# Retention and Fourier-mix kernel: the first batch's k and v loaded by casting transfers from GpSimd

## The chip, the cores and the metric

The kernel runs on one core of a Trainium2 chip. The metric is the device time of one execution in microseconds; lower is better. The core has five engines with their own instruction queues: TensorE (PE in the profile; PEld is its weight load), VectorE (DVE), ScalarE (ACT), GpSimd (POOL) and SyncE (SP), which here only issues transfers. Each runs its own list in order and waits on semaphores. Transfers go through 16 DMA engines, fed from a hardware queue (SP's) and a software queue (GpSimd's).

## The reference

Two stages. The first is a recurrence with decay over 768 steps, for 4 batches and 8 heads of width 64. The second adds the real part of a two-dimensional Fourier transform, normalizes, and runs an MLP of width 2048 with a residual.

```python
def _attn_ref(q, k, v):                       # (4, 8, 768, 64), float32
    gamma = 1.0 - 2.0 ** (-5.0 - np.arange(H))
    scale = 1.0 / np.sqrt(D)
    for t in range(S):
        state = gamma[None, :, None, None] * state + np.einsum('bhd,bhe->bhde', k[:, :, t], v[:, :, t])
        y[:, :, t] = scale * np.einsum('bhd,bhde->bhe', q[:, :, t], state)
    return y

def _moe_ref(x, w_ch1, w_ch2):                # x: (4, 768, 512)
    X = np.fft.fft(np.fft.fft(x, axis=1), axis=2)
    u = x + np.real(X).astype(np.float32)
    mu, var = np.mean(u, axis=-1, keepdims=True), ...
    un = (u - mu) / np.sqrt(var + 1e-06)
    return u + np.maximum(un @ w_ch1, 0.0) @ w_ch2
```

## The kernel before

**The recurrence in chunks.** The 768 steps are cut into 6 chunks of 128 (`NCH`, `P`), and heads are taken in pairs, four pairs to a batch, in the order 0, 1, 3, 2. Within a chunk the output is a masked product of q and k times v. Between chunks a 64 x 64 state per head is carried. The decay is split over the operands: `gkd` scales k by gamma^(127 - j) for row j of a chunk, `gq8` scales the output by gamma^(i + 1)/8 for row i. A product of q with the scaled k therefore carries a factor gamma^(128) too much between rows i and j, and the masked eviction (L471) multiplies by gamma^(-128) and by a mask of zeros and ones, `maskf`.

**A head pair of the first batch** goes through these units, each a small function:

- `load_unit` (L158) sends q, k and v of the pair from SP (L165), each 384 KB in float32, into the pool `inp` of 11 buffers. For q of the first two batches a partition holds six consecutive steps ("h (p c) d"), which makes rows of 1536 bytes in memory. For k and v a partition holds one step of each chunk ("h (c p) d"), which makes rows of 64 floats, 256 bytes. All four pairs' loads are issued at the start.
- `q0_unit` (L394) casts q to float16 on GpSimd. `k0_unit` (L402) scales and casts k into `kd` on GpSimd, one instruction a head; for the last pair the second head goes to ScalarE (L414). `v0_unit` (L418) casts v on GpSimd; for the last pair half of it goes to VectorE (L427).
- `t0_unit` (L430) transposes q (part 0) or the scaled k (part 1) on TensorE, six 128 x 128 transposes each, and `te_unit` (L442) copies the result out of PSUM on ScalarE.
- `am_unit` (L453) multiplies k and q per chunk (12 small matmuls), and `ae_unit` (L468) is the masked eviction on VectorE, four instructions a pair, into `atm`.
- `kv0_unit` (L477) multiplies the scaled k and v into the chunk states, `sc_unit` (L490) carries them through the chunks with one scan on VectorE.
- `yi_unit` and `yx_unit` (L501, L515) add both parts of the output in PSUM, and `x0_unit` (L531) writes them to `x` on ScalarE.

Between these stand units that build the Fourier tables: `ts_dve` and `td_dve` (L296, L305: three VectorE instructions each, L288 to L292), `t_act` and `csn_unit` on ScalarE. `filler` (L148) issues matmuls whose result is not used. `w1_unit` and `w2_unit` (L990, L998) load the MLP's weights: eight transfers from GpSimd which read float32 in rows of 512 floats and write float16.

**Order.** The order of the first batch is a list written by hand, `first_units` (L1037), and `pin` (L104) fixes it on every engine: an instruction can't pass the one ahead of it in the list on the same engine. GpSimd's constants (L198 to L222, L339 to L347) stand ahead of the whole list. After that the four batches' work is woven from streams with due times in units of one batch's MLP (`emit`, L1092), where only GpSimd's order is fixed. The order of SP's loads and transposes among these streams is set by a scheduler with a cost model, which knows when a buffer comes free.

**Later batches.** `cast_unit` (L361) does the casts on GpSimd for all later batches. The second batch's loads wait for the seventh weight transfer and for the matmuls of `h0_unit(1, 3)` (L166 to L171); loads of batches 2 and 3 wait for the matmuls of the pair a batch earlier (L172). Batches 2 and 3 transpose q and k by transfers on SP (L548, L550), and un as well (L916), so that SP's queue carries loads, transposes and the output's stores.

Of the kernel before, what the change touches and what calls it, by code (L numbers as in the profile page):

```python
# [18 lines left out]
P = 128  # L19
# [24 lines left out]
def kernel(  # L44
# [17 lines left out]
    inp = pool("inp", 11)  # L62
# [116 lines left out]

    for i in range(4):  # L180
        load_unit(0, i)()
# [5 lines left out]
    gexp = const.tile([P, 2, H], f32, tag="gexp")  # L187
    gq8, gkd = gexp[:, 0], gexp[:, 1]
# [15 lines left out]
    for h in range(H):  # L204
# [6 lines left out]
                            op0=ALU.mult)  # L211
    nc.scalar.activation(gexp, gexp, AF.Exp, bias=0.0, scale=1.0)
# [146 lines left out]
    at, q16_of, kd_of, v16_of, last_cast = {}, {}, {}, {}, {}  # L359

    def cast_unit(b, i):  # L361
        def run():
# [3 lines left out]
            v16 = vp.tile([P, NCH, 2, D], f16, tag="v16", name="v16")  # L366
            with ExitStack() as es:
# [14 lines left out]
                for h2 in range(2):  # L382
# [6 lines left out]
                    out=v16, in0=v32.rearrange("p h c d -> p c h d"), scalar1=1.0, scalar2=1.0,  # L389
# [11 lines left out]

    def k0_unit(i):  # L402
        def run():
            h0 = 2 * PAIR_ORDER[i]
            k32 = in_of.pop(("k", 0, i))
            kd = kd_of[0, i] = kp.tile([P, NCH, 2, D], f16, tag="kd16", name="kd16")
            nc.gpsimd.tensor_scalar(out=kd[:, :, 0, :], in0=k32[:, 0], scalar1=gkd[:, h0:h0 + 1],  # L407
                                    scalar2=1.0, op0=ALU.mult, op1=ALU.mult)
            if i < 3:
                nc.gpsimd.tensor_scalar(out=kd[:, :, 1, :], in0=k32[:, 1],  # L410
                                        scalar1=gkd[:, h0 + 1:h0 + 2], scalar2=1.0,
                                        op0=ALU.mult, op1=ALU.mult)
            else:
                nc.scalar.activation(kd[:, :, 1, :], k32[:, 1], AF.Copy, bias=0.0,  # L414
                                     scale=gkd[:, h0 + 1:h0 + 2])
        return run

    def v0_unit(i):  # L418
        def run():
            v32 = in_of.pop(("v", 0, i)).rearrange("p h c d -> p c h d")  # L420
            v16 = v16_of[0, i] = vp.tile([P, NCH, 2, D], f16, tag="v16", name="v16")
            n = NCH if i < 3 else 3
            last_cast[0, i] = nc.gpsimd.tensor_scalar(
                out=v16[:, 0:n], in0=v32[:, 0:n], scalar1=1.0, scalar2=1.0, op0=ALU.mult,
                op1=ALU.mult)
            if n < NCH:
                nc.vector.tensor_copy(v16[:, n:], v32[:, n:])  # L427
# [754 lines left out]
```

## Time and profile before

| What | Value |
|---|---|
| Time, median of 3 runs | 247.18 us (246.52 to 247.30) |
| Profiled execution, first to last instruction (its span) | 245.4 us |
| TensorE busy | 234.2 us, 95% of the span, 2024 matmuls |
| VectorE busy | 177.0 us, 72% |
| ScalarE busy | 124.2 us, 51% |
| GpSimd busy | 81.7 us, 33% |
| Bytes read from memory | 27.26 MB |
| SP queue | 94960 packets, 31.86 MB |
| GpSimd queue (weights) | 4224 packets, 4.19 MB |

The profiled execution has its own span; what lies around the span is in the time and not in the trace, so the time is compared with the span plus the difference, 1.8 us here. Busy time is the sum over an engine's instructions, each with its own start and end. A group of the timeline is printed as: start, length, engine, line, operation, output and input with shapes, count, and in brackets the idle time ahead of it with what ended it. The granted TensorE clock is 1.00 throughout.

### The profile page before, as it was taken

How to read it: one execution, taken by the hardware profiler on the slowest of the kernel's cores; microseconds unless marked ns; L12 is line 12 of the kernel's file. 1: busy time of each engine (PE TensorE's matmuls, PEld its weight loads, DVE VectorE, ACT ScalarE, POOL GpSimd, SP SyncE). 2: the span in 40 equal slices, each digit the busy share in tenths (PEclk: the TensorE clock that was granted, in tenths of full speed). 3: DMA queues.
4: the chain of work that ended last, by engine and by line, in shares of the span. 5: the costliest groups of instructions: out<-in, count | busy, mean ns of one | idle time of the engine just before them, and what ended most of it. 6: DMA issues, size and time to landing. Idle time of an engine off the chain costs nothing.

```text
span 245.4 us, 5309 instructions
## 1 busy us (share of the span) xinstructions
PE 234.2 (95%) x2024; PEld 143.8 (59%) x2024; DVE 177.0 (72%) x430; ACT 124.2 (51%) x276; POOL 81.7 (33%) x146
## 2 busy tenths in 40 slices
PE   6997899999999998999999999999999999999995
PEld 2454668956776655665567546655666455445543
DVE  8997957897897788996885748887895656424112
ACT  8798669587775434751247414742247317202500
POOL 6667601465600057690000646660002405000000
PEclk9999999999999999999999999999999999999999
DMA  8999999699999377999999667786200241221012
GB/s 173 256 260 140 204 195 205 164 245 230 291 229 222 75 168 165 191 181 137 256 272 214 116 141 203 129 120 139 87 1 0 45 151 21 47 85 43 0 45 85
DMA packets 99209, 36.39 MB, mean 148 GB/s; under 512 B 89840, under 2 KB 96240, under 8 KB 99184
## 3 DMA queue, kind: packets, MB, share of 16 engines
q1 hardware_dynamic: 94960, 31.86, 62.2%
q0 software_dynamic: 4224, 4.19, 10.7%
q8 instruction: 16, 0.26, 0.5%
q14 instruction: 9, 0.07, 0.1%
HBM read 27.26 MB, written 6.29 MB: 137 GB/s over the span
## 4 chain that ended last, share of the span: by engine, by line
PE 71%; DMA 7%; DVE 7%; POOL 4%; ACT 4%; SPq 3%; issue 1%; POOLq 0%; ACTq 0%; DVEq 0%
PE psc L979 30%; PE psh L936 25%; DMA k<-in_k_dram 5%; PE ps L736 3%; SPq L165 3%; PE wkA L600 3%; DMA q<-in_q_dram 2%; PE wkY L654 2%; PE pq L833 2%; PE wkY L650 1%; POOL u L870 1%; PE wkK L619 1%; ACT un L885 1%; DVE bst L889 1%; POOL kd L407 1%
## 5 line engine op out<-in xcount | busy, mean ns | idle before, releaser
L979 PE MATMUL psc<-w,ht 128*128 128x512 f16 (+2 forms) x400 | 89.3, 371 | 0.0
L936 PE MATMUL psh<-unT,w 128*128 128x384 f16 x448 | 81.6, 326 | 0.4 <-ACT ht L940 0.2
L979 PEld LDWEIGHTS <-ht 128*128 128x128 f16 x400 | 37.5, 98 | 36.5 <-issue 0.2
L936 PEld LDWEIGHTS <-w 128*128 128x128 f16 x448 | 42.3, 98 | 24.7 <-issue 1.4
L940 ACT ACTIVATE ht<-psh 128x384 f16<-128x384 f32 x64 | 30.9, 489 | 41.7 <-PE psh L936 41.1
L870 POOL TENSOR_TENSOR u<-u,x 128x256 f32<-128x256 f32 x21 | 13.3, 635 | 100.3 <-DVE u L840 91.0
L983 DVE SCALAR_TENSOR_TENSOR ob<-psc,stats,u 128x512 f32<-128x512 f32 (+2 forms) x25 | 18.1, 726 | 26.1 <-PE psc L979 26.0
L942 DVE TENSOR_SCALAR ht<-psh 128x384 f16<-128x384 f32 x48 | 26.2, 548 | 7.7 <-PE psh L936 7.4
L603 DVE TENSOR_TENSOR atm<-wkA,maskp 128x512 f16<-128x512 f32 x36 | 23.8, 681 | 1.6 <-PE wkA L600 1.6
L891 ACT ACTIVATE un<-u,stats 128x512 f16<-128x512 f32 x21 | 15.2, 722 | 16.7 <-DVE stats L890 12.1
L889 DVE BATCH_NORM_STATS2 bst<-u 128x6 f32<-128x512 f32 x21 | 14.6, 694 | 7.7 <-POOL u L872 7.6
L629 DVE SCALAR_TENSOR_TENSOR s<-s,gk,wkK 128x128 f16<-128x128 f16 x48 | 16.3, 341 | 3.7 <-ACT s L625 2.7
L662 ACT ACTIVATE x<-wkY,gexp 128x384 f16<-128x384 f32 x24 | 12.8, 581 | 8.0 <-PE wkY L654 8.0
L151 PE MATMUL wps<-ht 128*128 128x512 f16 x40 | 13.5, 444 | 2.2 <-POOL ht L202 2.2
L383 POOL TENSOR_SCALAR kd<-k,gexp 128x384 f16<-128x384 f32 x24 | 13.8, 585 | 3.6 <-DMA k<-in_k_dram 3.6
L872 POOL TENSOR_TENSOR u<-u,x 128x256 f32<-128x256 f32 x21 | 13.3, 635 | 3.0 <-DVE stats L890 3.0
L600 PE MATMUL wkA<-qTz,kT 128*128 128x256 f16 x72 | 13.4, 273 | 0.1
L835 ACT COPY qn<-pq 128x128 f32<-128x128 f32 x18 | 4.9, 272 | 13.6 <-PE pq L833 13.6
L953 PE MATMUL psh<-unT,w 128*128 128x128 f16 x192 | 11.5, 219 | 0.1
L953 PEld LDWEIGHTS <-w 128*128 128x128 f16 x192 | 11.0, 98 | 0.7 <-issue 0.5
L840 DVE SCALAR_TENSOR_TENSOR u<-pq,g,qn 128x256 f32<-128x256 f32 x18 | 8.5, 472 | 3.3 <-PE psh L936 2.5
L388 POOL TENSOR_SCALAR v<-v 128x768 f16<-128x768 f32 x12 | 10.0, 831 | 1.3 <-DMA v<-in_v_dram 1.3
(164 smaller groups left out, 315.6 us busy)
## 6 DMA issues: line engine op xcount, KB each, us to landing
q<-in_q_dram SPq DMA_DIRECT2D x16, 384.0 KB, 6.3
k<-in_k_dram SPq DMA_DIRECT2D x16, 384.0 KB, 5.6
v<-in_v_dram SPq DMA_DIRECT2D x16, 384.0 KB, 6.3
out_dram<-ob SPq DMA_DIRECT2D x23, 256.0 KB, 2.6
w<-in_moe_w_ch_dram POOLq DMA_DIRECT2D x8, 512.0 KB, 10.8
unT<-un SPq DMA_TRANSPOSE x15, 2.4
out_dram<-ob SPq DMA_DIRECT2D x1, 192.0 KB, 1.9
qTz<-q16z SPq DMA_TRANSPOSE x8, 3.9
```

The source lines that it names most:

```text
L600: mm = nc.tensor.matmul(wk[:, c2], st["kT"][:, c, :], st["qT"][:, :, c, :], start=True, stop=True)
L603: nc.vector.tensor_tensor(out=st["atm"][:, 2 * part:2 * part + 2], in0=wk, in1=maskp[:, PAIR_ORDER[i]].unsqueeze(1).to_broadcast([P, 2, 2, ...
L629: nc.vector.scalar_tensor_tensor(out=s16[:, c], in0=s16[:, c - 1], scalar=gk2[:, hp:hp + 1], in1=wk[:, c - c0], op0=ALU.mult, op1=ALU.add)
L870: nc.gpsimd.tensor_tensor(out=u[:, kb, 0:256], in0=u[:, kb, 0:256], in1=x[:, kb, 0, 1:257], op=ALU.add)
L889: nc.vector.bn_stats(bst, u[:, kb, :])
L891: una = nc.scalar.activation(un, u[:, kb, :], AF.Identity, bias=stats[:, kb, 0:1], scale=-1.0)
L936: nc.tensor.matmul(psh, w116[:, cb, fb * P:(fb + 1) * P], unT[:, cb, rt * 384:(rt + 1) * 384], start=(cb == 0), stop=(cb == 3))
L940: nc.scalar.activation(ht16[:, fb, :], psh, AF.Relu, bias=0.0, scale=-1.0)
L942: nc.vector.tensor_scalar(out=ht16[:, fb, :], in0=psh, scalar1=-1.0, scalar2=0.0, op0=ALU.mult, op1=ALU.max)
L953: mm = nc.tensor.matmul(psh[:, f], w116[:, cb, fb * P:(fb + 1) * P], unT[:, cb, kb * P:(kb + 1) * P], start=(cb == 0), stop=(cb == 3))
L979: nc.tensor.matmul(psc[:, c0:c1], ht16[:, fb, rb3 * P:(rb3 + 1) * P], w216[:, fb, c0:c1], start=(fb == 0), stop=(fb == NFB - 1))
L983: nc.vector.scalar_tensor_tensor(out=ob[:, c0:c1], in0=psc[:, c0:c1], scalar=lb[b]["st"][:, rb, 3:4], in1=lb[b]["u"][:, rb, c0:c1], op0=AL ...
```

## The change

- k and v of the first batch are no longer loaded by SP. Each is loaded by one transfer per head pair issued from GpSimd, which reads float32 and writes float16. SP loads q alone (`q_load`).
- These eight transfers stand in GpSimd's list: `kl_unit(0)`, `kl_unit(1)`, `vl_unit(0)` and `kl_unit(2)` ahead of everything else of `first_units`, the others between later units.
- GpSimd's scaling of k and cast of v are gone for this batch, with the parts that ScalarE and VectorE had. `k0_unit` now scales the float16 k into `kd` on VectorE, two instructions a pair, behind k's transposes in the list.
- `t0_unit` transposes the unscaled float16 k, head by head, twelve half-width transposes in place of six. The decay that the scaled k carried into the product is put into the masked eviction: its factor is now `gkm`, gamma^-(j + 1) for row j, one number a partition, in place of the constant gamma^(-128). `gkm` is a third row of the table of exponents `gexp`.
- v16 is laid out head, chunk, width in place of chunk, head, width, in all batches; the matmuls that read it are changed alike.
- The pool of float32 inputs goes from 11 to 8 buffers; a pool of 4 float16 buffers for k is new.

```diff
@@ -59,7 +59,8 @@
         return ctx.enter_context(tc.tile_pool(name=name, bufs=bufs, **kw))
 
     const = pool("const", 1)
-    inp = pool("inp", 11)
+    inp = pool("inp", 8)
+    kin = pool("kin", 4)
     vp = pool("vp", 4)
     kp = pool("kp", 3)
     tp = pool("tp", 2)
@@ -177,15 +178,20 @@
                 in_of[name, b, i] = t
         return run
 
+    def q_load(i):
+        h0 = 2 * PAIR_ORDER[i]
+        t = in_of["q", 0, i] = inp.tile([P, 2, NCH, D], f32, tag="in32", name="q32")
+        nc.sync.dma_start(t, q[0, h0:h0 + 2].rearrange("h (p c) d -> p h c d", p=P))
+
     for i in range(4):
-        load_unit(0, i)()
+        q_load(i)
 
 
     icol_i = const.tile([P, 8], i32, tag="icol_i")
     icol = const.tile([P, 8], f32, tag="icol")
     lgrow = const.tile([P, H], f32, tag="lgrow")
-    gexp = const.tile([P, 2, H], f32, tag="gexp")
-    gq8, gkd = gexp[:, 0], gexp[:, 1]
+    gexp = const.tile([P, 3, H], f32, tag="gexp")
+    gq8, gkd, gkm = gexp[:, 0], gexp[:, 1], gexp[:, 2]
     ident16 = const.tile([P, P], f16, tag="ident16")
     tmp = up.tile([P, NCH, DM], f32, tag="u32", name="tmp")
     tmp2 = up.tile([P, NCH, DM], f32, tag="u32", name="tmp2")
@@ -209,6 +215,8 @@
                             scalar2=float(math.log(0.125)), op0=ALU.mult, op1=ALU.add)
     nc.vector.tensor_scalar(out=gexp[:, 1], in0=lgrow, scalar1=icol[:, 5:6], scalar2=None,
                             op0=ALU.mult)
+    nc.vector.tensor_scalar(out=gexp[:, 2], in0=lgrow, scalar1=icol[:, 3:4], scalar2=-1.0,
+                            op0=ALU.mult, op1=ALU.mult)
     nc.scalar.activation(gexp, gexp, AF.Exp, bias=0.0, scale=1.0)
     for h2 in range(2):
         nc.scalar.activation(gk2[D * h2:D * h2 + D], lgrow[D * h2:D * h2 + D, h2:H:2], AF.Exp,
@@ -356,14 +364,14 @@
     x_edges(0)()
 
 
-    at, q16_of, kd_of, v16_of, last_cast = {}, {}, {}, {}, {}
+    at, q16_of, kd_of, v16_of, last_cast, k16_of = {}, {}, {}, {}, {}, {}
 
     def cast_unit(b, i):
         def run():
             h0 = 2 * PAIR_ORDER[i]
             q32, k32, v32 = (in_of.pop((n, b, i)) for n in "qkv")
             kd = kp.tile([P, NCH, 2, D], f16, tag="kd16", name="kd16")
-            v16 = vp.tile([P, NCH, 2, D], f16, tag="v16", name="v16")
+            v16 = vp.tile([P, 2, NCH, D], f16, tag="v16", name="v16")
             with ExitStack() as es:
                 if b < NPE:
                     if (b, i - 1) in last_cast:
@@ -386,7 +394,7 @@
                     if b < NPE:
                         es.enter_context(tc.issue_after(kc.ins))
                 last_cast[b, i] = nc.gpsimd.tensor_scalar(
-                    out=v16, in0=v32.rearrange("p h c d -> p c h d"), scalar1=1.0, scalar2=1.0,
+                    out=v16, in0=v32, scalar1=1.0, scalar2=1.0,
                     op0=ALU.mult, op1=ALU.mult)
             q16_of[b, i], kd_of[b, i], v16_of[b, i] = q16, kd, v16
         return run
@@ -399,32 +407,31 @@
                 "p h c d -> p c h d"), scalar1=1.0, scalar2=1.0, op0=ALU.mult, op1=ALU.mult)
         return run
 
+    def kl_unit(i):
+        def run():
+            h0 = 2 * PAIR_ORDER[i]
+            k16_of[i] = kin.tile([P, 2, NCH, D], f16, tag="k16", name="k16")
+            nc.gpsimd.dma_start(k16_of[i],
+                                k[0, h0:h0 + 2].rearrange("h (c p) d -> p h c d", p=P))
+        return run
+
     def k0_unit(i):
         def run():
             h0 = 2 * PAIR_ORDER[i]
-            k32 = in_of.pop(("k", 0, i))
             kd = kd_of[0, i] = kp.tile([P, NCH, 2, D], f16, tag="kd16", name="kd16")
-            nc.gpsimd.tensor_scalar(out=kd[:, :, 0, :], in0=k32[:, 0], scalar1=gkd[:, h0:h0 + 1],
-                                    scalar2=1.0, op0=ALU.mult, op1=ALU.mult)
-            if i < 3:
-                nc.gpsimd.tensor_scalar(out=kd[:, :, 1, :], in0=k32[:, 1],
-                                        scalar1=gkd[:, h0 + 1:h0 + 2], scalar2=1.0,
-                                        op0=ALU.mult, op1=ALU.mult)
-            else:
-                nc.scalar.activation(kd[:, :, 1, :], k32[:, 1], AF.Copy, bias=0.0,
-                                     scale=gkd[:, h0 + 1:h0 + 2])
-        return run
-
-    def v0_unit(i):
-        def run():
-            v32 = in_of.pop(("v", 0, i)).rearrange("p h c d -> p c h d")
-            v16 = v16_of[0, i] = vp.tile([P, NCH, 2, D], f16, tag="v16", name="v16")
-            n = NCH if i < 3 else 3
-            last_cast[0, i] = nc.gpsimd.tensor_scalar(
-                out=v16[:, 0:n], in0=v32[:, 0:n], scalar1=1.0, scalar2=1.0, op0=ALU.mult,
-                op1=ALU.mult)
-            if n < NCH:
-                nc.vector.tensor_copy(v16[:, n:], v32[:, n:])
+            for h2 in range(2):
+                nc.vector.tensor_scalar(out=kd[:, :, h2, :], in0=k16_of[i][:, h2],
+                                        scalar1=gkd[:, h0 + h2:h0 + h2 + 1], scalar2=None,
+                                        op0=ALU.mult)
+        return run
+
+    def vl_unit(i):
+        def run():
+            h0 = 2 * PAIR_ORDER[i]
+            v16 = v16_of[0, i] = vp.tile([P, 2, NCH, D], f16, tag="v16", name="v16")
+            last_cast[0, i] = nc.gpsimd.dma_start(
+                v16,
+                v[0, h0:h0 + 2].rearrange("h (c p) d -> p h c d", p=P))
         return run
 
     def t0_unit(i, part):
@@ -432,11 +439,16 @@
             if part == 0:
                 at[0, i] = dict(kT=tp.tile([P, NCH, P], f16, tag="kT", name="kT"),
                                 qT=qts[i % 2][:, 0])
-            src = (q16_of, kd_of)[part][0, i]
             tq = at[0, i]["tq", part] = ps_g.tile([P, NCH, P], f16, tag="g", name="tq",
                                                   padded_shape=[P, 8, P])
             for c in range(NCH):
-                nc.tensor.transpose(tq[:, c, :], src[:, c].rearrange("p a b -> p (a b)"), ident16)
+                if part:
+                    for h2 in range(2):
+                        nc.tensor.transpose(tq[D * h2:D * h2 + D, c, :], k16_of[i][:, h2, c, :],
+                                            ident16)
+                else:
+                    nc.tensor.transpose(
+                        tq[:, c, :], q16_of[0, i][:, c].rearrange("p a b -> p (a b)"), ident16)
         return run
 
     def te_unit(i, part):
@@ -470,7 +482,7 @@
             st = at[0, i]
             nc.vector.scalar_tensor_tensor(
                 out=st["atm"][:, 3 * half:3 * half + 3, h2, :], in0=st["wk", half][h2],
-                scalar=float(gam[2 * PAIR_ORDER[i] + h2] ** (-P)),
+                scalar=gkm[:, 2 * PAIR_ORDER[i] + h2:2 * PAIR_ORDER[i] + h2 + 1],
                 in1=maskf.unsqueeze(1).to_broadcast([P, 3, P]), op0=ALU.mult, op1=ALU.mult)
         return run
 
@@ -484,7 +496,7 @@
             for c in range(NCH - 1):
                 for h2 in range(2):
                     nc.tensor.matmul(wk[64 * h2:64 * h2 + 64, :, c], kd[:, c, h2, :],
-                                     v16[:, c, h2, :], start=True, stop=True)
+                                     v16[:, h2, c, :], start=True, stop=True)
         return run
 
     def sc_unit(i):
...
@@ -617,7 +629,7 @@
                 wk = ps_g.tile([P, 3, P], f32, tag="g", name="wkK", padded_shape=[P, 4, P])
                 for c in range(c0, c0 + n):
                     nc.tensor.matmul(wk[:, c - c0, :], kd[:, c].rearrange("p a b -> p (a b)"),
-                                     v16[:, c].rearrange("p a b -> p (a b)"),
+                                     v16[:, :, c, :],
                                      start=True, stop=True)
                 for c in range(c0, c0 + n):
                     if c == 0:
...
@@ -1051,26 +1063,26 @@
         std = ((0, 0), (0, 1), (1, 0), (1, 1))
         heads = ((0, 0), (1, 0), (0, 1), (1, 1))
         o = PAIR_ORDER
-        un = [ts_dve(0), gk_unit(o[0]), gk_unit(o[1]), t_act(0, 0), t_act(0, 1),
+        un = [kl_unit(0), kl_unit(1), vl_unit(0), kl_unit(2), ts_dve(0), gk_unit(o[0]), gk_unit(o[1]), t_act(0, 0), t_act(0, 1),
               q0_unit(0), t0_unit(0, 0), filler(4), ts_dve(1), te_unit(0, 0), t_act(0, 2),
-              k0_unit(0), t0_unit(0, 1), filler(3), te_unit(0, 1), ts_dve(2), td_dve(0), t_act(1, 0),
-              t_act(1, 1), t_act(1, 2), v0_unit(0)]
+              t0_unit(0, 1), k0_unit(0), vl_unit(1), filler(3), te_unit(0, 1), ts_dve(2), td_dve(0), t_act(1, 0),
+              t_act(1, 1), t_act(1, 2), kl_unit(3)]
         un += a(0) + [filler(1), kv0_unit(0)] + e(0, *std) + [sc_unit(0)]
         un += [q0_unit(1), t0_unit(1, 0), te_unit(1, 0), t_act(2, 0), t_act(2, 1), filler(4),
-               k0_unit(1), t0_unit(1, 1), te_unit(1, 1)]
-        un += y(0) + [parity_consts, yx_unit(0), filler(2)] + x(0) + [t_act(2, 2), v0_unit(1),
+               k0_unit(1), t0_unit(1, 1), te_unit(1, 1), vl_unit(2)]
+        un += y(0) + [parity_consts, yx_unit(0), filler(2)] + x(0) + [t_act(2, 2),
                                                                      half_ids]
         un += a(1) + [csn_unit(0), filler(1), kv0_unit(1)] + e(1, *std) + [sc_unit(1)]
-        un += [q0_unit(2), t0_unit(2, 0), te_unit(2, 0), csn_unit(1), filler(3), k0_unit(2),
+        un += [q0_unit(2), t0_unit(2, 0), te_unit(2, 0), csn_unit(1), filler(3), k0_unit(2), vl_unit(3),
                t0_unit(2, 1), te_unit(2, 1)]
         un += y(1) + [td_dve(1), yx_unit(1), filler(2)] + x(1) + [
-            gk_unit(o[2]), t_act(3, 0), t_act(3, 1), v0_unit(2)]
+            gk_unit(o[2]), t_act(3, 0), t_act(3, 1)]
         un += a(2) + [filler(1), kv0_unit(2)] + e(2, *std) + [sc_unit(2), t_act(3, 2),
                                                               csn_unit(2)]
         un += [q0_unit(3), w1_unit(0), t0_unit(3, 0), te_unit(3, 0), filler(3)] + y(2)
         un += [fold_s(0, 0, 258, 0, 1), g0_unit(0, (0,)), k0_unit(3), t0_unit(3, 1),
                te_unit(3, 1), yx_unit(2), gk_unit(o[3]), x0_unit(2, 0), x0_unit(2, 1),
-               t_act(4, 0), t_act(4, 1), filler(2), v0_unit(3)]
+               t_act(4, 0), t_act(4, 1), filler(2)]
         un += [w1_unit(g) for g in range(1, 4)] + [w2_unit(g) for g in range(4)]
         un += a(3) + e(3, (0, 0), (1, 0)) + [kv0_unit(3), filler(4), sc_unit(3), t_act(4, 2)]
         un += e(3, (0, 1), (1, 1))
```

More of the change, by code (lines that the diff above doesn't have):

```diff
@@ L509, in run @@
             for c in range(NCH):
-                nc.tensor.matmul(y[:, c, :], atm[:, c, h2, :], v16[:, c, h2, :],
+                nc.tensor.matmul(y[:, c, :], atm[:, c, h2, :], v16[:, h2, c, :],
                                  start=first and c == 0, stop=not first and c == NCH - 1,
@@ L653, in run @@
                 for c in range(NCH):
-                    nc.tensor.matmul(yk[h2][:, c, :], atm[:, c, h2, :], v16[:, c, h2, :],
+                    nc.tensor.matmul(yk[h2][:, c, :], atm[:, c, h2, :], v16[:, h2, c, :],
                                      start=False, stop=(c == NCH - 1), skip_group_check=True)
```

## The prediction

> **What bounds the kernel now.** I read the page first, then the chain of waits, then the first 36 us engine by engine. The page's row of busy time gives TensorE 95% of the span, but that includes filler matmuls: up to about 36 us TensorE waits for short chains through the other engines, and from there to the end it runs the MLP back to back. So whatever delays the first batch's head pairs moves the rest with it. The later loads do not absorb it either: batch 1's first load is issued at 44.89 us, right behind the 128th of the L953 matmuls, which it waits for. The chain of waits in order of time (start, length, what) shows this stage:
>
> ```profile
> 9.61 5.65 DMA k<-in_k_dram
> 15.34 0.59 POOL kd L407
> 15.93 0.57 POOL kd L410
> 16.55 0.51 PE tq L439 x6
> 20.47 0.90 POOL w L993
> 21.41 1.28 POOL kd L407
> 24.55 0.60 DVE atm L471 x2
> 27.22 0.55 DVE xab L679 x2
> ```
>
> Until 20 us it is the loads: a k transfer, its GpSimd scaling, its transposes. The last pair's k also sits behind a weight transfer's issue on GpSimd (20.47). The windows view (start:end, length, busy of PE, PEld, DVE, ACT, POOL) has one line from each pair's first masked eviction to the next pair's:
>
> ```profile
> 9.90:14.00 4.10, 3.76 (x62) 2.35 (x58) 3.76 (x12) 3.50 (x8) 2.78 (x6) 1.00 1.25 258
> 14.00:18.70 4.70, 4.14 (x70) 2.47 (x63) 4.14 (x8) 4.29 (x9) 2.61 (x4) 1.00 1.26 254
> 18.70:24.50 5.80, 4.13 (x68) 2.53 (x62) 4.85 (x10) 4.71 (x11) 4.82 (x6) 1.00 0.92 135
> ```
>
> DVE has little left: its idle time in the timeline, from 9.88 to 27.2 us, is 0.25, 0.46, 0.92 and 0.07 us between groups. A stall put into DVE here can hardly be made up. GpSimd's timeline is where the change lands:
>
> ```profile
> 3.98 0.14 POOL L347 MEMSET x<- 128x48 f16 x1
> 4.18 0.83 POOL L398 TENSOR_SCALAR q16z<-q 128x768 f16<-128x768 f32 x1
> 6.07 0.60 POOL L407 TENSOR_SCALAR kd<-k,gexp 128x384 f16<-128x384 f32 x1 [1.05 <-DMA k<-in_k_dram]
> 20.41 0.96 POOL L993 DMA_DIRECT2D w<-in_moe_w_ch_dram  x1
> 23.12 2.29 POOL L993 DMA_DIRECT2D w<-in_moe_w_ch_dram  x3
> ```
>
> GpSimd is busy with constants until 4.12 us, then casts q of pair 0. SP had sent k of pair 0 at 1.32 us, so that it was scaled from 6.07. A weight transfer costs GpSimd 0.75 to 0.96 us to issue.
>
> **The transfers.** k and v move in rows of 64 floats (256 B), 1536 to a pair. In the DMA view of 4 to 20 us the rate falls to 218 GB/s where k and v run alone and peaks at 343 to 369 where q is among them: 393 KB take 1.80 us for k or v, about 1.1 for q, so 4.7 us a pair and 18.9 in all, from 2 to 20.9 us.
>
> ```profile
> DMA packets 11979, 4.03 MB, mean 252 GB/s; under 512 B 11210, under 2 KB 11978, under 8 KB 11978
> ```
>
> The rows read stay the same. I take 1.80 us a tensor for the casting queue too. Lower bound: the weights' 205 GB/s written is 196 KB in 0.96 us. Upper: twice the SP row, 3.6 us, if half-size writes go at half the rate. 1.80 is the row with the same rows read.
>
> **Removed from GpSimd**: per pair k's scaling (2 x 0.59) and v's cast (0.83 to 0.98), some 7.3 us before 23 us. **Removed elsewhere**: the ACT half of kd (0.62, off the chain), the DVE cast of v (0.54). SP loses eight loads; its four q loads (0.46 us an issue, 4.5 us of data) are through by about 7 us, so no q cast waits for data any more.
>
> **Added to GpSimd**: eight issues of 1536 rows. The trace has none that size. Lower end: 0.75 us, if the issue does not grow with rows (SP's does not: 0.46 us for q with 256 rows, 0.45 for k with 1536). Upper end: three times the weights' 512 rows, 3 x 0.77 = 2.3 us. I take 1.25, a third of the way up: the row nearest in kind is the weights', the only pair of rows with different counts shows no growth, but on SP.
>
> Four of these (k0, k1, v0, k2) stand ahead of the first q cast: 4.15 + 4 x 1.25 = 9.15, cast done at 9.98 instead of 5.01. From q's cast to the first masked eviction the old timeline has 9.88 - 5.01 = 4.87 us, of which some 0.6 were waiting for DVE's tables and the k scaling; I count 0.6 (transposes) + 1.75 (four fillers) + 0.8 (k's transposes) + 0.8 (ACT copy) + 0.3 = 4.25, and 0.3 more for twelve half-width k transposes in place of six (six took 0.51 to 0.67; ten to twelve of the small L464 and L486 take 0.47 to 0.51, so the bounds are 0 and 0.6). First masked eviction: 9.98 + 4.55 = 14.5 instead of 9.88, **+4.6**.
>
> DVE is not what is late at that point, but it stalls too: its first k scaling now stands ahead of the tables of L288 to L292. A software transfer's data start 2.4 us after its issue starts (weights: issue at 20.41, the rate leaves its floor at 22.9), so k0 lands about 4.15 + 2.4 + 1.8 + 0.4 = 8.75; DVE would be there at 5.4. Scaling 0.5, then tables:
>
> ```profile
> 5.80 0.42 DVE L288 TENSOR_SCALAR tmp<-tmp,icoln 128x386 f32<-128x386 f32 x1
> 6.25 0.63 DVE L290 TENSOR_SCALAR tmp<-tmp 128x386 f32<-128x386 f32 x1
> 6.91 0.82 DVE L292 SCALAR_TENSOR_TENSOR tmp<-tmp,icol,tmp 128x386 f32<-128x386 f32 x1
> 8.86 1.10 DVE L292 SCALAR_TENSOR_TENSOR tmp<-tmp,icol,tmp 128x257 f32<-128x257 f32 x1
> 9.88 1.94 DVE L471 SCALAR_TENSOR_TENSOR atm<-wkA,maskf 128x384 f16<-128x384 f32 x4
> ```
>
> Without GpSimd casts beside them the same lines take 0.36 (L290, at 2.93 us) and 0.62 (L292), so the six need 2.5 us instead of 4.1: done at 11.75, covered by the 14.5.
>
> **Added to DVE later**: per pair two f16 scalings of 128x384. Nearest rows: f16 copies of 384 in 0.21 us (L752), small f16 scalings in 0.27 (L254): 0.45 a pair, bounds 0.3 and 1.0. Pair by pair, idle taken out, 0.45 put in: 14.5 + (4.16 - 0.25 + 0.45) = 18.9; + (4.67 - 0.46 + 0.45 - 0.2 for faster tables) = 23.3; + (5.84 - 0.92 - 0.54 + 0.45) = 28.15; + 2.65 = 30.8 against 27.2, where the fold xab follows. **+3.6 us.** v of the last pair lands about 22.4, before its use near 28. The weights start at 4.15 + 8 x 1.25 + 4 x 0.83 + 0.56 = 18.0 instead of 20.41: no stall.
>
> **At nothing**: the third row of exponents (about 0.13 us on DVE at 2 us, under GpSimd's constants); a scalar operand in the eviction in place of a number; v16's new order (L373 casts in the plain order, L398 in the permuted one: 0.83 both). The load pool shrinks from 11 to 8 buffers: batches 2 and 3 may then send a load only when the tile eight earlier is cast. The loads this holds back (v of pair 2 on) are cast 10 us later than their new issue, and that is the cover; gone, it costs one load ahead of a transpose on SP, 1.8 us a batch.
>
> The profiled span was 245.4; the median of the runs is 1.8 above it. 245.4 + 3.6 = 249.0 in the trace, 250.8 as time. Each microsecond of issue moves it by four: at 0.75 the DVE stall nearly meets the q path and it is +1.6 (248.8); at 2.3 it is +7.8 (255.0).
>
> **Two rules of the Trainium skill.** "DMA: Bandwidth & Descriptors" (Anatomy of one DMA) says that many descriptors can be emitted before generating them costs more; by it the issue would stay near 0.75 and the time near 248.8. "SBUF — State Buffer" (SBUF: two separate sides) says that descriptors of GpSimd transfers wait while DVE holds the shared port in a two-port mode. That speaks against the change; the stretched L290 (0.36 to 0.86 us beside GpSimd casts) agrees that the two engines get in each other's way, and no row shows it for an issue.
>
> **Rivals.**
> 1. *Cheap issue and quick data: faster.* Nothing proves that an issue costs 0.75 where DVE is idle. At 0.3 us q is cast by 6.2; at 0.96 us a tensor k0 lands at 4.15 + 0.3 + 1.4 + 0.96 + 0.4 = 7.2, DVE's tables end 0.5 + 2.5 later, at 10.2: first eviction +0.3, then the 1.0 of idle and v cast recovered: -0.7, and up to -1.5 if the fillers run at their later 0.26 us each: 246.5 to 245.7. It decides from issues under 0.45 us on. For: 2.9 us of waiting for k's data by GpSimd go. Against: the weights' rows.
> 2. *The casting queue is the bound.* At 3.0 us a tensor v of the last pair lands at 6.55 + 24 + 0.4 = 31 and its use follows at 31 instead of 28: +6, 253. For: 128 B written at a time. Against: the weights move 410 GB/s read.
> 3. *The buffers.* The loads behind the transposes cost 1.8 us in each of batches 2 and 3 on top: 254.4. For: unT's third transpose at 143.99 is needed at 147. Against: ten microseconds of slack for each load.
> 4. *It shifts nothing*: q's delay is taken up, k's earlier arrival for the last pair (17 instead of 20) pays the rest: 247.2. It needs an issue of 0.5 us.
>
> **Chances.** Forecast 0.52, rival 2 0.13, rival 3 0.08, rival 4 0.10, rival 1 0.17. A change under 0.3% (0.74 us) can't be told from none: faster 0.17, same 0.10, slower 0.73. The forecast's own range is 248.8 to 255.0. The whole range is 246.0 to 255.2: it takes in most of rivals 1 and 4 and the upper bound of the issue.
>
> **What would show it.** The first issue row of k on GpSimd (1.25 us each), the first q cast at 9.2 instead of 4.18, an idle DVE before its first k scaling until 8 to 9 us, the first L471 group at 14.5 and the first fold near 30.8, the L936 rows 3.6 us later throughout. It is wrong if the issues take under 0.5 us, if the first eviction is before 11 us, or if the first fold comes late and the end does not.

## The result and the profile after

The changed kernel takes 253.43 us (median of 3 runs, 252.64 to 255.13), against 247.18 before: 1.027 times, 95% interval 1.0224 to 1.0316. Slower by 6.25 us; 250.8 was forecast. The profiled execution took 252.64 us with a span of 250.8, again 1.8 apart, so the trace holds 5.4 us of the loss. The other two runs had spans of 253.2 and 251.6 at a mean granted clock of 0.993, where the profiled one had 1.000.

**Where it went.** Three marks cut the span. The first is the first load of batch 1 on SP's queue, behind the first batch's pairs. The second is the first run of 48 `psc` matmuls (the MLP's second product, L979 before and L991 after) in both chains of waits. The third is the end.

| Stretch | Before | After | Difference |
|---|---|---|---|
| Start to the first load of batch 1 | 44.89 us | 48.32 us | +3.43 |
| From there to the 48 `psc` matmuls | 91.76 us | 93.69 us | +1.93 |
| From there to the end | 108.75 us | 108.8 us | 0 |

The forecast has the first row (+3.6) and nothing for the second. The rows are of one execution each.

**The first stretch.** GpSimd's timeline after:

```profile
3.79 2.26 POOL L414 DMA_DIRECT2D k<-in_k_dram  x2
...
8.07 0.97 POOL L406 TENSOR_SCALAR q16z<-q 128x768 f16<-128x768 f32 x1
...
16.53 3.08 POOL L1005 DMA_DIRECT2D w<-in_moe_w_ch_dram  x4
```

An issue of 1536 rows costs GpSimd 1.03 to 1.24 us, 1.06 in the median of k's. Four of them, 4.28 us from 3.79 on, put the first q cast at 8.07 instead of 4.18. But GpSimd is through with the first batch early: the weights start at 16.53 instead of 20.41. VectorE's timeline, ahead of the first masked eviction (now L483):

```profile
6.28 0.97 DVE L298 TENSOR_SCALAR tmp<-tmp 128x386 f32<-128x386 f32 x1
...
9.83 0.69 DVE L423 TENSOR_SCALAR kd<-k,gexp 128x384 f16<-128x384 f16 x2 [1.48 <-DMA k<-in_k_dram]
...
13.54 0.49 DVE L300 SCALAR_TENSOR_TENSOR tmp<-tmp,icol,tmp 128x257 f32<-128x257 f32 x1
13.94 2.19 DVE L483 SCALAR_TENSOR_TENSOR atm<-wkA,gexp,maskf 128x384 f16<-128x384 f32 x4
...
30.62 0.62 DVE L691 TENSOR_TENSOR xab<-x 128x390 f16<-128x390 f16 x2
```

VectorE does the first tables beside GpSimd's issues, and L298 (L290 before, 0.36 us where it ran alone) takes 0.97. So VectorE comes to its first k scaling at 8.35, waits 1.48 us for k, and only then does six more table instructions, which end where the first eviction starts. The eviction waits for nothing that a bracket shows. The four evictions take 2.19 us where they took 1.94. The fold of the last pair starts at 30.62 instead of 27.13.

The DMA view of 4 to 20 us (forty slices of 0.4 us), before and then after:

```profile
GB/s 290 243 217 218 218 218 248 234 346 343 285 260 218 216 218 220 218 220 257 257 369 303 287 242 216 216 218 218 218 229 271 288 350 280 280 248 226 224 220 219
```

```profile
GB/s 342 131 200 250 319 392 346 290 228 162 151 155 156 151 156 156 156 158 155 154 157 156 156 156 156 154 155 154 138 97 64 66 112 143 147 131 18 28 105 169
```

The casting transfers hold a level of 151 to 158 GB/s as written, 156 in most slices: 196,608 bytes in 1.26 us, 312 GB/s as read. SP's uncast transfers of the same rows went at 218 (1.80 us). The first batch's loads end about 18.4 us, where the last one's slices fall from 131 to 18, instead of 20.9.

**The second stretch.** The windows view of 105 to 125 us (start:end, length, then busy time and count of PE, PEld, DVE, ACT and POOL, granted clock, DMA share, GB/s), before and after:

```profile
105.00:125.00 20.00, 20.00 (x194) 12.29 (x192) 16.39 (x36) 6.30 (x15) 5.87 (x11) 1.00 1.05 199
```

```profile
105.00:125.00 20.00, 18.23 (x168) 10.91 (x166) 14.35 (x35) 7.59 (x18) 7.29 (x13) 1.00 1.05 175
```

TensorE was never idle there and now misses 1.77 us. Its timeline and ScalarE's, after:

```profile
117.23 0.39 PE L612 MATMUL wkA<-qTz,kT 128*128 128x256 f16 x2 [0.66 <-DMA kT<-kd]
117.90 0.72 ACT L903 ACTIVATE un<-u,stats 128x512 f16<-128x512 f32 x1 [6.26 <-DMA unT<-un]
119.59 0.39 PE L612 MATMUL wkA<-qTz,kT 128*128 128x256 f16 x2 [1.11 <-DVE s L641]
```

ScalarE waits 6.26 us for a transpose of `un` that SP sends, then copies the state for a VectorE scan (L641), and TensorE waits 1.11 us for that scan. The other 0.66 of the 1.77 is a direct wait for kT, another transpose on SP's queue. SP's queue, before and then after:

```profile
103.31 3.44 SPq L916 DMA_TRANSPOSE unT<-un  x2
106.85 1.44 SPq L548 DMA_TRANSPOSE qTz<-q16z  x1
```

```profile
109.33 3.46 SPq L560 DMA_TRANSPOSE qTz<-q16z  x1
112.88 1.23 SPq L562 DMA_TRANSPOSE kT<-kd  x1
114.21 3.68 SPq L928 DMA_TRANSPOSE unT<-un  x2
```

`un` was transposed ahead of q and k of the next pair, at 103.31. It now goes behind them, at 114.21. That is 10.9 us later, while the work around it is 3.4 later. The scheduler plans SP's order, and it planned it for a pool of 8 buffers.

### The profile page after: what moved, and what is told of

Read it like the earlier page. It is cut to its first block, busy times and chain, and to the rows that moved or that the text cites. A ratio compares the mean times of both kernels' runs of the same rounds, so it can differ in the third digit from the quotient of the medians.

```text
span 250.8 us, 5348 instructions
## 1 busy us (share of the span) xinstructions
PE 236.0 (94%) x2048; PEld 144.5 (58%) x2048; DVE 180.8 (72%) x438; ACT 123.2 (49%) x275; POOL 82.2 (33%) x143
## 4 chain that ended last, share of the span: by engine, by line
PE 45%; DVE 3%; POOL 2%; ACT 1%; issue 1%; POOLq 0%; ACTq 0%
PE psc L991 23%; PE psh L948 16%; PE ps L748 2%; PE wkA L612 1%; PE wkY L666 1%; DVE u L852 1%; POOL u L882 1%; DVE bst L901 1%; PE wkY L662 1%; PE pq L845 1%; POOL u L884 1%; DVE s L641 0%; ACT qn L847 0%; PE wkK L631 0%; ACT un L903 0%
## 5 line engine op out<-in xcount | busy, mean ns | idle before, releaser
L991 PE MATMUL psc<-w,ht 128*128 128x512 f16 (+2 forms) x400 | 89.3, 370 | 0.0
L991 PEld LDWEIGHTS <-ht 128*128 128x128 f16 x400 | 37.6, 98 | 36.4 <-issue 0.2
L952 ACT ACTIVATE ht<-psh 128x384 f16<-128x384 f32 x64 | 30.8, 489 | 42.6 <-PE psh L948 42.1
L641 DVE SCALAR_TENSOR_TENSOR s<-s,gk,wkK 128x128 f16<-128x128 f16 x48 | 16.4, 342 | 8.1 <-ACT s L637 7.1
L612 PE MATMUL wkA<-qTz,kT 128*128 128x256 f16 x72 | 13.4, 273 | 1.9 <-DVE s L641 1.1
L612 PEld LDWEIGHTS <-kT 128*128 128x128 f16 x72 | 6.6, 98 | 8.3 <-DVE s L641 2.0
```

Source lines behind the costliest of these rows:

```text
L612: mm = nc.tensor.matmul(wk[:, c2], st["kT"][:, c, :], st["qT"][:, :, c, :], start=True, stop=True)
L641: nc.vector.scalar_tensor_tensor(out=s16[:, c], in0=s16[:, c - 1], scalar=gk2[:, hp:hp + 1], in1=wk[:, c - c0], op0=ALU.mult, op1=ALU.add)
L952: nc.scalar.activation(ht16[:, fb, :], psh, AF.Relu, bias=0.0, scale=-1.0)
L991: nc.tensor.matmul(psc[:, c0:c1], ht16[:, fb, rb3 * P:(rb3 + 1) * P], w216[:, fb, c0:c1], start=(fb == 0), stop=(fb == NFB - 1))
```

## The experiments

**1. The smaller pool alone, in the kernel before.**

```
-    inp = pool("inp", 11)
+    inp = pool("inp", 8)
```

> The kernel before with one edit: 8 buffers in the pool of float32 inputs in place of 11. Theory A (the pool costs some 2 us of its own: with 8 buffers the loads of batch 2 are held back, and SP issues un's transposes behind them): span 246.9 to 248.4 against 245.4, the first fold (DVE xab) still at 27.1 to 27.3 us, the two unT transposes of batch 2 issued near 110 instead of 103.3, and ScalarE waiting over 4 us for unT there. Theory B (the extra 2 us come from the later start of the whole, not from the pool): span 245.0 to 245.8 and unT at 103 to 104.

252.59 us (250.69 to 254.26), 1.0222 times before (1.0166 to 1.0279). The first stretch is as before, with the first load of batch 1 at 44.68. The second takes 97.10 us instead of 91.76. Its windows view and TensorE's timeline:

```profile
105.00:125.00 20.00, 16.61 (x130) 8.81 (x127) 11.57 (x29) 4.89 (x11) 5.46 (x10) 0.91 0.95 184
```

```profile
117.68 0.39 PE L600 MATMUL wkA<-qTz,kT 128*128 128x256 f16 x2 [3.12 <-DVE s L629]
117.90 1.64 PE L979 MATMUL psc<-w,ht 128*128 128x512 f16 x4
```

SP's queue and ScalarE's timeline:

```profile
111.81 3.45 SPq L916 DMA_TRANSPOSE unT<-un  x2
115.98 0.72 ACT L891 ACTIVATE un<-u,stats 128x512 f16<-128x512 f32 x1 [7.78 <-DMA unT<-un]
```

The pool alone makes the place of the changed kernel's loss: `unT` on SP at 111.81 instead of 103.31, 7.78 us of waiting for it on ScalarE, 3.12 on TensorE. It is dearer than I expected (span 251.2 against 246.9 to 248.4), since behind the gap the granted clock falls: four `psc` matmuls take 1.64 us where they take 1.03 elsewhere. Of the 5.34 us of the stretch some 3.3 are waits and 1.8 such longer matmuls. The one run with a clock of 1.000 has a span of 248.9.

**2. The change with all 11 buffers.** Two pairs' float16 k share one buffer of `inp`, so `kin` is not needed.

```
-    inp = pool("inp", 8)
-    kin = pool("kin", 4)
+    inp = pool("inp", 11)
...
-            k16_of[i] = kin.tile([P, 2, NCH, D], f16, tag="k16", name="k16")
+            if i % 2 == 0:
+                kk[0] = inp.tile([P, 2, NCH, D], f32, tag="in32", ...
+            k16_of[i] = kk[0][:, i % 2]
```

> The changed kernel with 11 buffers in the pool of float32 inputs again; two pairs' float16 k share one of them, so that no other memory is needed. Theory A (pool): the first fold stays at 30.4 to 30.8, the span goes from 250.8 to 248.6 to 249.2, and the SP order of batch 2 is that of the kernel before. Theory B: span 250.4 to 251.2.

251.41 us (250.79 to 251.99), 1.0169 times before (1.0141 to 1.0197), 2.0 below the change as it is, with no overlap of the intervals. The second stretch takes 91.73 us, as before the change, and 105 to 125 us is full again:

```profile
105.00:125.00 20.00, 20.00 (x183) 12.26 (x181) 16.68 (x40) 8.57 (x21) 8.44 (x15) 1.00 1.06 195
```

```profile
108.18 2.88 SPq L932 DMA_TRANSPOSE unT<-un  x2
111.17 1.43 SPq L564 DMA_TRANSPOSE qTz<-q16z  x1
```

SP sends `unT` ahead of the next pair's q again. The other runs agree: in every profile with 8 buffers (the changed kernel, experiments 1, 3, 4 and 8) this stretch takes 93.69 to 97.10 us, in every one with 11 (the kernel before, experiments 2, 5, 6, 7, 9 and 10) 91.56 to 92.00.

The profiled span, 250.0, is above the 248.6 to 249.2 that I expected (two other runs have 249.0), because the first stretch came out 1.2 us longer than in the changed kernel (49.53):

```profile
9.98 1.18 DVE L427 TENSOR_SCALAR kd<-k16x,gexp 128x384 f16<-128x384 f16 x2 [1.63 <-DMA k16x<-in_k_dram]
15.34 2.19 DVE L487 SCALAR_TENSOR_TENSOR atm<-wkA,gexp,maskf 128x384 f16<-128x384 f32 x4
```

VectorE's first k scaling took 1.18 us instead of 0.69, the tables behind it were stretched too, and the last of them ends where the eviction starts. The granted clock was 0.76 from 7 to 14 us, but that did not move the eviction: the `wkA` matmuls start at 13.15, where they start at 13.30 in the changed kernel. Why the same list runs 1.2 us longer here is open.

**3. A number in the eviction instead of the scalar operand.** The output lacks the column factor, since every row gets the same number.

```
-                scalar=gkm[:, 2 * PAIR_ORDER[i] + h2:2 * PAIR_ORDER[i] + h2 + 1],
+                scalar=float(gam[2 * PAIR_ORDER[i] + h2] ** (-P)),
```

> The changed kernel with the constant gamma^(-128) in the first batch's masked eviction, as before the change; the decay per row is left out of the product of q and k, for its time alone. Theory A (a scalar read per partition costs each of the 16 evictions about 60 ns: groups of four took 2.19 us in place of 1.94): groups of four at 1.94 to 1.96, the first fold 0.7 to 1.0 us earlier, at 29.6 to 29.9. Theory B (the longer groups come from GpSimd's issues beside them): groups of four stay at 2.15 to 2.2, the fold at 30.5 to 30.7.

One run, 254.06 us. The groups of four take 1.95 us again, so the operand costs 0.06 us an instruction, 0.24 a pair and 1.0 in all sixteen. The fold does not come earlier: it starts at 31.35, and the span is 252.1. k of the first pair landed at 10.58 instead of 9.83 and its scaling took 1.47 us, so the first eviction came at 15.41. The price is settled; what it is worth at the end is not, as the spread of the first pair is larger.

**4. Wide rows for k and v.** The loads take the steps in another order, six to a partition, so what is computed has its rows permuted.

```
-                                k[0, h0:h0 + 2].rearrange("h (c p) d -> p h c d", p=P))
+                                k[0, h0:h0 + 2].rearrange("h (p c) d -> p h c d", p=P))
```

> The changed kernel with k and v loaded in rows of 1536 bytes (a partition holds six consecutive steps), 256 rows a pair in place of 1536; the steps are then in the wrong order, so the output is not the reference's. Theory A (the issue on GpSimd grows with the rows: 0.76 us at 512, 1.05 at 1536): the issue takes 0.65 to 0.75, the first q cast starts near 6.6 to 6.9 instead of 8.07, k0 lands by 8.3, the first eviction at 12.0 to 13.0. Theory B (the issue is set by DVE's work beside it, not by rows): the issues stay at 1.0 to 1.1 and the q cast at 8.0.

One run, 252.90 us. GpSimd's timeline, and VectorE's:

```profile
3.79 1.64 POOL L414 DMA_DIRECT2D k<-in_k_dram  x2
...
6.91 0.85 POOL L406 TENSOR_SCALAR q16z<-q 128x768 f16<-128x768 f32 x1
```

```profile
9.96 0.55 DVE L423 TENSOR_SCALAR kd<-k,gexp 128x384 f16<-128x384 f16 x2 [3.29 <-ACT ssp L328]
13.54 2.19 DVE L483 SCALAR_TENSOR_TENSOR atm<-wkA,gexp,maskf 128x384 f16<-128x384 f32 x4
```

The issue falls to 0.72 us in the median (0.92 for the first) and the q cast comes 1.16 earlier, but the first eviction only 0.40, and the fold (30.03) 0.59. VectorE waits 3.29 us for its first k scaling. The bracket names ScalarE's L328, whose result the k scaling doesn't read; in the changed kernel, with the same order, the k scaling ran ahead of it (9.83, where L328 ended at 11.20). I read it as the landing of k. From there to the eviction VectorE is busy without a break, while the `wkA` matmuls end at 12.53. So the q cast alone does not set the first eviction: a VectorE queue that stands behind k's landing does as well. That this part of the forecast ("each microsecond of issue moves it by four") fails is shown by these rows, not by the 0.40 itself: with one and the same list the first eviction came at 13.94, 14.34, 15.34 and 15.41 (the changed kernel, experiments 8, 2 and 3).

**5. The first k scaling behind the tables** (on top of experiment 2).

```
-              t0_unit(0, 1), k0_unit(0), vl_unit(1), filler(3), te_unit(0, 1), ts_dve(2), td_dve(0), t_act(1, 0),
+              t0_unit(0, 1), vl_unit(1), filler(3), te_unit(0, 1), ts_dve(2), td_dve(0), k0_unit(0), t_act(1, 0),
```

> The changed kernel with 11 input buffers and the first pair's k scaling moved behind the tables in VectorE's list (behind the fourth table instead of ahead of the third). Theory A (VectorE's wait for k0 sets the first eviction, since the tables stand behind it): VectorE does not idle between 8.4 and 9.9 us, the tables end near 12 us, the first eviction starts at 13.3 to 13.8 instead of 15.3 (13.9 in the run with 8 buffers), the span is 248.4 to 248.9. Theory B (the q cast behind four issues sets it): the first eviction stays above 14.5 and the span at 249.6 to 250.2.

251.59 us (250.73 to 251.80), 1.016 times before (1.0133 to 1.0188): no gain over experiment 2. VectorE's timeline:

```profile
12.55 0.68 DVE L427 TENSOR_SCALAR kd<-k16x,gexp 128x384 f16<-128x384 f16 x2
14.35 2.19 DVE L487 SCALAR_TENSOR_TENSOR atm<-wkA,gexp,maskf 128x384 f16<-128x384 f32 x4 [1.11 <-PE wkA L480]
```

VectorE is through at 13.23 and now it waits, 1.11 us, for TensorE. The q chain was right behind, and it ran slowly: TensorE had been idle 4.21 us ahead of the first q transposes, its granted clock over the first 15 us was 0.78, and the twelve `wkA` matmuls took 0.82 us instead of 0.51. The eviction falls between the two expectations, and the span (249.7) is that of theory B: neither had both chains nearly level, and that is what this shows.

**6. q's cast ahead of the issues, and the k scaling behind the tables** (on top of experiment 2).

```
-        un = [kl_unit(0), kl_unit(1), vl_unit(0), kl_unit(2), ts_dve(0), ...
+        un = [q0_unit(0), kl_unit(0), kl_unit(1), vl_unit(0), kl_unit(2), ts_dve(0), ...
```

> As inp11_k0_behind, and the first q cast ahead of the four issues on GpSimd. Theory A (both chains, q's cast and k0's landing, end together, and k0's start behind GpSimd's constants is what is left): q cast at 4.2, k0's issue at 5.0 and its landing at 10.8 to 11.2, first eviction at 12.8 to 13.4, span 247.8 to 248.4. Theory B (the q cast behind four issues sets it): first eviction at 9.9 to 11.0, span 246.0 to 246.8.

250.66 us (249.56 to 252.01), 1.0134 times before (1.0093 to 1.0175); span 247.7. TensorE's timeline and VectorE's:

```profile
5.49 1.47 PE L152 MATMUL wps<-ht 128*128 128x512 f16 x4
9.65 0.77 PE L451 MATMUL tq<-ident,k16x 128*64 128x128 f16 x12 [2.69 <-DMA k16x<-in_k_dram]
10.35 1.46 PE L152 MATMUL wps<-ht 128*128 128x512 f16 x3
11.74 0.82 PE L480 MATMUL wkA<-qTz,kT 64*128 64x128 f16 x12
```

```profile
10.77 1.44 DVE L427 TENSOR_SCALAR kd<-k16x,gexp 128x384 f16<-128x384 f16 x2
12.35 2.19 DVE L487 SCALAR_TENSOR_TENSOR atm<-wkA,gexp,maskf 128x384 f16<-128x384 f32 x4
```

The q cast is at 3.99, the first eviction at 12.35 (12.8 to 13.4 was expected), the fold at 29.28 instead of 31.82 in experiment 2. Both chains have to be shortened for the first eviction to move. They end level again: TensorE waits 2.69 us, to 9.65, for k, although k's issue moved to 4.77, and VectorE, busy without a break, is through with its tables and the k scaling at 12.21.

**7. More fillers across that wait** (experiment 6 with `filler(14)` in place of `filler(4)`).

> As inp11_q_first with 14 filler matmuls in place of 4 behind the first q transposes, which fill TensorE's 2.7 us of waiting for k0. Theory A (after such a gap the granted clock falls for some us, by chance of where the gap lies, and that is the scatter of 247.7 to 250.2 between runs): the granted clock is 1.00 in every run, the first eviction stays at 12.1 to 12.6, spans agree within 0.5 us at 246.9 to 247.7. Theory B (the scatter has nothing to do with the gap): clocks of 0.985 to 0.993 and spans over 248.4 in some runs.

249.38 us (249.31 to 249.85), 1.0093 times before (1.0075 to 1.0112). TensorE's timeline:

```profile
10.26 0.82 PE L152 MATMUL wps<-ht 128*128 128x512 f16 x3
11.22 0.51 PE L480 MATMUL wkA<-qTz,kT 64*128 64x128 f16 x12
```

Three fillers take 0.82 us where they took 1.46 behind the gap, and `wkA` 0.51 instead of 0.82. The eviction hardly moves (12.20), as VectorE is busy up to it. The spread over the runs falls from 2.45 to 0.54 us. The spans are 247.4, 248.0, 247.6 and 247.5 at clocks of 1.000, 1.000, 0.999 and 1.000; in experiment 6 they were 247.7, 249.2, 250.2 and 248.4 at 0.993, 0.986, 0.985 and 0.993. In experiment 6 the slowest run has the lowest clock. So most of the scatter of experiment 6 comes from a clock that falls after TensorE stands idle, and the fillers close the gap; runs of nearly the same clock there still differ by 0.7 and 1.0 us. With the buffers back, q first and the gap closed, the changed kernel is still 2.1 us above the kernel before: its first eviction comes at 12.20 where it came at 9.88.

**8. A third buffer for `un`** (on top of the change, to see whether the two buffers of `un` carry SP's lateness to ScalarE).

```
+    unp = pool("unp", 3)
...
-            un = up.tile([P, 2, 257], f16, tag="un16", name="un16").rearrange(
+            un = unp.tile([P, 2, 257], f16, tag="un16", name="un16").rearrange(
```

> The changed kernel (8 input buffers) with three buffers for the normalized rows un in place of two; SP's list keeps unT's transposes behind those of q and k of pair 2. Theory A (ScalarE stands still for the un buffer that SP's late transposes hold, and with it the state copy that VectorE and TensorE wait for): ScalarE's wait for unT in batch 2 goes from 6.3 us to under 1, and the stretch from batch 1's first load to the first 48 psc matmuls is 91.8 to 92.6 us instead of 93.7. Theory B (the transfers themselves, k's transposes above all, are what is late): the stretch stays at 93.3 or more.

254.96 us (253.77 to 255.68), 1.0308 times before (1.0281 to 1.0334). ScalarE's wait is gone and nothing is won. SP's queue and TensorE's timeline:

```profile
116.39 4.75 SPq L929 DMA_TRANSPOSE unT<-un  x3
119.17 0.39 PE L613 MATMUL wkA<-qTz,kT 128*128 128x256 f16 x2 [1.58 <-DMA kT<-kd]
128.53 0.38 PE L613 MATMUL wkA<-qTz,kT 128*128 128x256 f16 x2 [1.57 <-DMA qTz<-q16z]
```

SP now has three `unT` transposes in a row at 116.39 and sends kT at 121.67 and qT at 123.63. The second stretch takes 95.43 us, where theory A had 91.8 to 92.6. So a third buffer for `un` does not bring the loss back: SP's late queue reaches TensorE through kT and qT as well, as 0.66 us of it already did in the changed kernel. What the buffer would be worth with SP's order held is not shown, since this edit moved SP's order again: the third `unT` went ahead of kT.

**9. Casting transfers for the last two pairs alone** (on the kernel before: k and v of pairs 2 and 3; k still scaled on GpSimd before its transposes, 11 buffers, no scalar operand; the parts that ScalarE and VectorE had of the last pair's casts go to GpSimd or fall away, and the first weight transfer goes behind the last pair's casts).

```
-              q0_unit(0), t0_unit(0, 0), ...
+              q0_unit(0), kl_unit(2), t0_unit(0, 0), ...
...
-        un += [q0_unit(1), t0_unit(1, 0), ...
+        un += [q0_unit(1), vl_unit(2), t0_unit(1, 0), ...
...
-                                                                     half_ids]
+                                                                     kl_unit(3), half_ids]
...
-            gk_unit(o[2]), t_act(3, 0), t_act(3, 1), v0_unit(2)]
+            gk_unit(o[2]), t_act(3, 0), t_act(3, 1), vl_unit(3)]
```

> The kernel before (11 buffers, scaled k transposed, constant in the eviction) with casting transfers for the last two pairs only: q, k, v of pairs 0 and 1 and q of pairs 2 and 3 by SP, k and v of pairs 2 and 3 by GpSimd, whose issues stand where it waited for data; k is scaled on GpSimd. Theory A (a casting transfer moves a tensor in 1.27 us instead of 1.80 and frees the v casts; started where nothing waits for it, it is a gain): pair 3's scaled k is ready by 19.5 to 20.5 instead of 22.7, the first fold at 25.6 to 26.4 instead of 27.2, span 244.0 to 244.8. Theory B (issues beside VectorE's two-port work cost as much as they free): first fold at 26.8 to 28.0, span 245.0 to 246.3.

247.71 us (247.4 to 249.14, 10 runs), 1.0034 times before (1.0014 to 1.0054): the outcome of theory B (span 245.7, last fold at 27.18). GpSimd's timeline:

```profile
13.80 0.83 POOL L450 TENSOR_SCALAR v<-v 128x768 f16<-128x768 f32 x1 [1.72 <-DMA v<-in_v_dram]
14.57 1.06 POOL L435 DMA_DIRECT2D k16x<-in_k_dram  x1
```

The casting transfers run beside SP's, v of pair 1 lands 1.4 us later than before, and the issue of k for the last pair stands behind the cast that waits for it. The third pair's first eviction (pair 2, counted from 0) comes at 20.49 instead of 18.71.

**10. That issue ahead of the waiting cast.**

```
-        un += y(0) + [...] + x(0) + [t_act(2, 2), v0_unit(1), kl_unit(3), half_ids]
+        un += y(0) + [...] + x(0) + [t_act(2, 2), kl_unit(3), half_ids, v0_unit(1)]
```

> As hybrid, with the issue of pair 3's k and two small instructions moved into GpSimd's 1.7 us of waiting for pair 1's v. Theory A (GpSimd's order alone cost pair 2 its gain): pair 2's first eviction at 18.7 to 19.3 instead of 20.5, first fold of the late half at 26.0 to 26.6 instead of 27.2, span 244.4 to 245.0. Theory B (beside the casting queue SP's own loads land later, v of pair 1 at 13.8 instead of 12.4, and that eats it): span 245.2 to 246.0.

246.46 us (245.93 to 246.92, 7 runs), 0.9971 times before (0.9957 to 0.9984): faster than both kernels, if by 0.8 us.

```profile
12.07 1.06 POOL L435 DMA_DIRECT2D k16x<-in_k_dram  x1
13.85 0.83 POOL L450 TENSOR_SCALAR v<-v 128x768 f16<-128x768 f32 x1
```

The issue fills the wait, pair 2's eviction comes at 19.20 and the last fold at 25.88 instead of 27.13. The span is 244.5. Of the 1.25 us won at the fold the end keeps 0.9.

## Why the prediction was right in kind and short in size

The direction, and that the first batch's delay moves the rest with it, were right. The sum of the first stretch was right as well (+3.6 forecast, +3.43 in the profiled execution), but partly by terms that cancel, and partly by luck: with the same list the stretch took 4.1 to 4.6 us more than before in the profiles of experiments 2, 3 and 8.

- **The issue** was taken as 1.25 us, and is 1.06 in the median. The q cast came at 8.07, not 9.15, as the issues also began at 3.79 instead of 4.15. The forecast's lower end, 0.75 without growth by rows, falls: 256 rows take 0.72 (experiment 4). Rivals 1 and 4 needed 0.5 or less, and fall too.
- **The casting queue** was taken as 1.80 us a tensor, and is 1.26, between the bounds of 0.96 and 3.6. Rival 2 falls with it.
- **"DVE is not what is late at that point"** was wrong. k landed at 9.83 instead of 8.75, although the queue was faster than taken. The tables, expected without GpSimd's casts beside them at 2.5 us, took 3.5, beside GpSimd's issues and q cast, and ended where the first eviction starts, at 13.94 instead of 11.75. The q chain ends almost with them (experiment 5). The 14.5 was therefore 0.56 too late, by two errors of opposite sign. In the forecast I had cited the Trainium skill's "SBUF — State Buffer" (SBUF: two separate sides) for descriptors held up by VectorE. The trace shows VectorE stretched beside the issues, 0.36 to 0.97 us for L298. That the issues were held up too doesn't show: v's at 9.00, for most of which VectorE stood idle, took 1.06 us like those beside VectorE's work.
- **k's scaling** was taken as 0.45 us a pair, and is 0.54 to 0.79. **The scalar operand**, costed at nothing, is 0.24 a pair (experiment 3).
- **The pairs** were sized at 4.4, 4.4, 4.85 and 2.65 us, and took 4.35, 4.85, 4.67 and 2.81. The fold came at 30.62, forecast 30.8.
- **What failed is the term at nothing for the pool from 11 to 8.** The forecast named the cover, that the loads held back have ten microseconds of slack, and priced its loss at 1.8 us a batch. The cover was the wrong one. The loads came no later for their casts: from 50 us on GpSimd waits 7.2 us in all for them, 7.0 before. But with 8 buffers the order of the other transfers in SP's queue changed, and `unT`, which had no such slack, went behind a pair's transposes. That costs 1.93 us in the trace. With the buffers back it is gone (91.73), and the median falls by 2.0 (experiment 2), though that figure holds the scatter of the first stretch as well. Alone in the kernel before it costs 5.6 (252.59 against 247.02), slower matmuls behind the gap included. Rival 3 had the edit and the queue, but with a price for each of batches 2 and 3 and with the loads ahead of the transposes; the loss is in one place.
- **The rest of the median.** The forecast and the pool make 250.8 + 1.9 = 252.7, close to the profiled 252.64. The median is 0.8 above that, and it and the slowest run have a clock of 0.993. Two causes fit, and neither was tried on the changed kernel itself. One is the idle TensorE, 4.21 us ahead of the first q transposes: experiment 7 shows what such a gap is worth in another list. The other is VectorE: with the same list the last fold came at 30.62 in this profile, but at 31.82, 31.35 and 31.27 in those of experiments 2, 3 and 8, of which the last two have a clock of 1.000. So the 0.8 stays open.

Of what the forecast said would show it, the issue rows (1.06 us for 1.25), the idle VectorE, the eviction and the fold are there, and the q cast is a microsecond early. "3.6 us later throughout" holds as far as batch 2's pairs and fails behind them.

Why k of the first pair lands between 9.65 and 10.58 us whether its issue starts at 3.79 or 4.77 is open. Until about 7.6 us SP's q transfers fill the DMA view, which would account for it, but no run took them away.

## What to carry to other kernels

A pool's size is part of the order of the queue that fills it. Where loads and other transfers share one queue in order, take away buffers only after asking which other transfer of that queue moves when a load waits, and test that edit by itself: it is one line.

A transfer that casts takes work off an engine and puts the issue, here over 1 us, in its place. Put such issues where the engine would wait, not ahead of the first thing that starts the chain: the transfers for two pairs of four, in the right places, with all the buffers and with k still scaled ahead of its transposes, gave -0.8 us where the whole edit gave +6.25.

## What the runs showed of the hardware

- GpSimd's issue of a transfer grows with rows, but over a floor: 0.72 us for 256 rows (experiment 4), 0.75 for the weights' 512, 1.06 for 1536, and the first of a kernel about 0.2 more.
- Casting transfers of 256-byte rows moved 312 GB/s as read, SP's uncast ones 218. Rows of half the size in writing did not make them slower.
- VectorE's tables took up to 2.7 times as long (0.36 to 0.97 us) beside GpSimd's issues, not only beside its casts. It isn't every instruction: L300 took its 0.62 us at 12.27, beside an issue, and in experiment 6 L298 itself took 0.36 at 6.20, beside one. What decides is open.
- The granted clock fell after TensorE had been idle for 2.69 to 4.21 us, to 0.76 over 7 to 14 us in experiment 2 and 0.78 over the first 15 us in experiment 5. The column doesn't show it in every execution: the changed kernel's profiled run and experiment 8's have the same gap and 1.00 throughout, and yet in experiment 8 the first `wkA` matmuls take 0.82 us instead of 0.51, as in experiment 5. The rows of the matmuls are the surer sign. The first ones of an execution are long with and without a gap (four fillers in 1.91 us in the kernel before, 1.03 later). The Trainium skill's "TensorE: Matmul & The Clock Gate" (Part 1: The HAM clock gate) states half rate after an idle window of about 3.4 us, in windows that run freely, so that it varies between runs. The dips and their scatter agree. The 2.69 us gap of experiment 6 is shorter than the window and had one too (0.993 over the span, three fillers in 1.46 us for 0.82); there the measurement decides.
